# Attention logits computed once, and the probabilities turned by DMA transposes

## The chip, the cores and the metric

The kernel runs on one core of a Trainium2 chip. The metric is device microseconds of that core for one launch; lower is better. Each kernel is run several times, and the median is compared. The profiles show one execution each, in microseconds from its first instruction. The engines are TensorE (PE, with its weight loads as PEld), VectorE (DVE), ScalarE (ACT), GpSimd (POOL) and SyncE (SP), which in this kernel issues all DMA transfers. A queue name with a q (SPq) is an engine's instruction queue.

## What is computed

The reference mixes, per token, a memory-augmented attention and a SwiGLU feed-forward part with a sigmoid gate. There are 2048 tokens, 576 model dimensions, 32 heads of 18 dimensions and 4608 hidden dimensions. Attention is causal within each of four segments of 512 tokens; a running state carries earlier segments.

```python
for s in range(N):                      # N = 4 segments of L = 512
    logits = jnp.einsum("bhqd,bhkd->bhqk", qs, ks) * scale + mask
    p = _softmax(logits, axis=-1)
    a_dot = jnp.einsum("bhqk,bhkd->bhqd", p, vs)
    num = jnp.einsum("bhld,bhde->bhle", pq, M)
    den = jnp.einsum("bhld,bhd->bhl", pq, z)[..., None] + 1e-6
    outs.append(g * num / den + (1.0 - g) * a_dot)
    M = M + jnp.einsum("bhld,bhle->bhde", pk, vs)
    z = z + jnp.einsum("bhld->bhd", pk)
a = o @ wo                              # o: the segments' outputs together
b = (silu(x @ w_gate) * (x @ w_up)) @ w_down
return gate * a + (1 - gate) * b        # gate = sigmoid(x . gate_w)
```

Inputs and output are float32. The kernel reaches this precision with split operands: a number is carried as a high term and one or two low terms of a narrower type, and the products of the terms are added in PSUM.

## The kernel before

A first stage (to about 230 us) makes q, k and v, the state and its reads. It writes q and k, each as three bf16 terms, into a DRAM tensor `stk`, and v into `vd`. The last stage (from about 1710 us) multiplies with `wo` and mixes. Between them runs the feed-forward part, twice through 36 blocks of hidden units: `seven` (L1034 and L1037) makes gate and up products, `down_group` (L893) the down product of three blocks at a time. In the first half the split weights are made (`w_make`) and stored to DRAM (`wc`, `dc`); in the second they are fetched again (`w_fetch` at L703, `d_fetch`).

The softmax attention is woven into these two halves. `att_gen` is a generator; each of its steps (`tau`) issues a few instructions of several stages of a pipeline, and `beat`, called between the feed-forward's products, lets it do a step whenever a credit (`TICK`) has reached one. The order of every engine is the order in which the program issues; there is no scheduler.

A unit `u` is two heads of one segment. Its causal logits, in blocks of 128 x 128, fill five PSUM banks (`SPLAN`, `TPLAN`). `stack_loads` brings its q and k from `stk` with the terms laid out one under another on 108 partitions (`KR`), so that one matmul adds all products of terms. The pipeline of a unit:

- `s_bank` (L727, L734), step 5u+n: logits with queries on the partitions, two heads, and DVE's maximum of each row of a query block into `mb`. With the fifth bank DVE splits the eight columns of maxima, less a shift, into three bf16 terms `mq` (L740 to L743).
- `m_tr` (L748, L750): a matmul with the identity turns `mq`, ACT copies it to `mt`; SP stores it to DRAM (`mxd`, L830) and loads it back as three more rows of `qst` (`row_load`, L193). The same rows of `kst` hold -1.
- `t_bank` (L769, L773, L781), 12 steps behind `s_bank` (`TL`): the logits again, with keys on the partitions and the maxima subtracted by the three rows, 111 partitions deep; ACT takes the exponential of the whole bank, POOL zeroes the masked half of the diagonal blocks.
- two steps later (`PL`) DVE casts the bank to fp16 (`p1`, L861) and POOL subtracts for the low term (`p2`, L863).
- `pv_step` (L798, L800): 40 matmuls per unit, each with a 128 x 128 block of `p1` or `p2` as weights and v's three (two) bf16 terms and the column of ones as moving operand, into one bank; DVE adds the terms (L805).
- `o_step` divides by the row sum and stores the result to `atd`.

The three banks 5, 6 and 7 (`ts_tile`) serve `s_bank`, `t_bank`, `m_tr` and the unit's output in turn. `qst` and `kst` have four buffers each (`NST`), since a unit's q and k are needed until its `t_bank`.

Of the kernel before, what the change touches and what calls it, by code (L numbers as in the profile page):

```python
# [37 lines left out]
NST = 4  # L38
TL = 12
PL = 2  # L40
VL = 3
# [22 lines left out]
def gated_mix(ctx, tc, xT, xrest, wf, wfr, wfh, wd, wv, wo, beta, cmask, ident, bmask, out):  # L64
# [11 lines left out]
    mxd = dram.tile([2 * NB, 3, 8, P], BF, name="mxd")  # L76
# [96 lines left out]
    VP, accs, cur, unit, ms, mts, mbs = {}, {}, {}, {}, {}, {}, []  # L173
# [17 lines left out]

    def row_load(u):
        nc.sync.dma_start(qst[u % NST][KR:KR + 3].rearrange("z j (i n) -> z (j i) n", n=P), mxd[u])  # L193

# [75 lines left out]
    with ExitStack() as st:  # L270
# [314 lines left out]
        for s in range(NSEG):  # L585
# [41 lines left out]
            if s == 3:  # L627
# [4 lines left out]
                for i in range(NST):  # L632
                    if i < 2:
                        qst.append(kq.tile([P, 2, L], BF, name=f"qst{i}"))
                    if i < NST - 1:
                        kst.append(kq.tile([P, 2, L], BF, name=f"kst{i}"))
# [9 lines left out]
            for n in range(8):  # L646
# [10 lines left out]
                else:  # L657
                    if n == 4:
                        wraw_of[1] = [w_load(1, u) for u in range(2)]
                    if n < 2:  # L660
                        first_sum(6, n)
                    elif n < 6:
                        if n < 4:
                            nc.gpsimd.memset(f32(rhs[n - 2][96:]), 0.0)
                        if 3 <= n < 5:
                            r_fetch(n - 3)
                        if n - 2 < len(kst):
                            nc.gpsimd.memset(kst[n - 2], -1.0)
# [13 lines left out]
    with ExitStack() as st:  # L682
# [26 lines left out]
        kst.append(kp.tile([P, 2, L], BF, name=f"kst{NST - 1}", bufs=1))  # L709
        for i in range(2, NST):  # L710
            qst.append(kp.tile([P, 2, L], BF, name=f"qst{i}", bufs=1))
        defer(8, lambda: nc.gpsimd.memset(kst[NST - 1], -1.0))
        idb = kp.tile([P, P], BF, name="idb", bufs=1)
        defer(9, lambda: nc.gpsimd.tensor_copy(idb, idt))
        mqs = [kp.tile([P, P], BF, name=f"mq{i}", bufs=1) for i in range(2)]
        for i in range(2):
            defer(9 + i, lambda i=i: nc.gpsimd.memset(mqs[i], 0.0))
        SPLAN = [[(0, 0, 3)], [(0, 1, 3)], [(384, 0, 0), (0, 0, 2)], [(384, 1, 0), (0, 1, 2)], [(0, 0, 1), (256, 1, 1)]]

        def s_bank(u, n):  # L720
            qs, ks = qst[u % NST], kst[u % NST]
            m = mbs[u % 2]
            bank = SPLAN[n]
            t = ts_tile()
            for c, pr, i in bank:
# [3 lines left out]
                yield  # L729
            for c, pr, i in bank:  # L730
# [3 lines left out]
                nc.vector.tensor_tensor_reduce(scr[:, :w], t[:, c:c + w], cm[:, L - w:L], 1.0, -3.0e38,  # L734
                                               OP.add, OP.max, m[:, k:k + 1])
            if n == 4:
                mq = mqs[u % 2][:, :24].rearrange("p (z q) -> p z q", q=8)
                mr = kp.tile([P, 8], F32, name="mr")
                c = -SHIFT / SCALE
                nc.vector.tensor_scalar_add(mq[:, 0], m, c)  # L740
                nc.vector.scalar_tensor_tensor(mr, m, c, mq[:, 0], op0=OP.add, op1=OP.subtract)
                nc.vector.tensor_copy(mq[:, 1], mr)
                nc.vector.tensor_sub(mq[:, 2], mr, mq[:, 1])  # L743
            yield

        def m_tr(u):
            tr = ts_tile()
            nc.tensor.matmul(tr[:, :P], mqs[u % 2], idb, start=True, stop=True)  # L748
            mt = mts[u] = kp.tile([24, P], BF, name="mt")
            nc.scalar.activation(mt, tr[:24, :P], AF.Copy)  # L750

        def blk(pr, j, i):
            if j == 0:
                return pr, P * i
            if j == 1:
                return 2 + pr, P * (i - 1)
            if j == 3:
                return 2 + pr, 384
            return 4, 256 * pr + P * (i - 2)

        TPLAN = [[(0, 0)], [(1, 0)], [(0, 1), (0, 3)], [(1, 3), (1, 1)], [(0, 2), (1, 2)]]

        def t_bank(u, k):
            qs, ks = qst[u % NST], kst[u % NST]
            t = ts_tile()
            for pr, j in TPLAN[k]:
                _, c = blk(pr, j, j)
                w = L - P * j
                nc.tensor.matmul(t[:, c:c + w], ks[:KR + 3, pr, P * j:P * j + P], qs[:KR + 3, pr, P * j:L],  # L769
                                 start=True, stop=True)  # L770
                yield
            pe = ap.tile([P, L], F32, name="pe", bufs=4)
            nc.scalar.activation(pe, t, AF.Exp, scale=SCALE)  # L773
            if k < 2:
                d = pe[:, 0:P]
                pat = [[1, P]]
            else:
                st_ = 384 if k < 4 else 256
                d = bass.AP(tensor=pe.tensor, offset=pe.offset, ap=[pe.ap[0], [st_, 2], [1, P]])
                pat = [[0, 2], [1, P]]  # L780
            nc.gpsimd.affine_select(d, d, pattern=pat, compare_op=OP.is_ge, fill=0.0, base=0, channel_multiplier=-1)  # L781
            cur[5 * u + k] = pe
            yield

        def pv_step(z):
            u, k = divmod(z, 5)
            g, hf = divmod(u, 2)
            s, b = divmod(u, 16)
            if k == 0:
                unit[u] = ts_tile([P, 2, 4, 3 * E])  # L790
# [32 lines left out]
        def att_gen():  # L823
            N = 10 * NB
            for tau in range(N + TL + VL + 5):
# [26 lines left out]
                if u < 2 * NB:  # L852
                    runs.append(s_bank(u, n))
# [378 lines left out]
```

## Time and profile before

| | us |
|---|---|
| three runs | 1804.73, 1805.08, 1808.49 |
| median | 1805.08 |
| span of the profiled execution | 1803.0 |

The page of the profile gives, per engine, busy time and its share of the span; the chain that ended last, followed back from the last instruction; and the costliest groups of instructions. A row of a group reads: line, engine, operation, output<-input with partitions and elements, count; then busy time and mean duration in ns of one; then the idle time of the engine just before such instructions, and what ended it. Views of a window give the busy time of each engine in it (with the number of instructions in brackets), the granted TensorE clock, the mean share of the 16 DMA engines that was in use, and what they moved.

### The profile page before, as it was taken

How to read it: one execution, taken by the hardware profiler on the slowest of the kernel's cores; microseconds unless marked ns; L12 is line 12 of the kernel's file. 1: busy time of each engine (PE TensorE's matmuls, PEld its weight loads, DVE VectorE, ACT ScalarE, POOL GpSimd, SP SyncE). 2: the span in 40 equal slices, each digit the busy share in tenths (PEclk: the TensorE clock that was granted, in tenths of full speed). 3: DMA queues.
4: the chain of work that ended last, by engine and by line, in shares of the span. 5: the costliest groups of instructions: out<-in, count | busy, mean ns of one | idle time of the engine just before them, and what ended most of it. 6: DMA issues, size and time to landing. Idle time of an engine off the chain costs nothing.

```text
span 1803.0 us, 36363 instructions
## 1 busy us (share of the span) xinstructions
PE 1779.1 (99%) x12444; PEld 1529.7 (85%) x12444; DVE 1269.7 (70%) x3257; ACT 960.0 (53%) x1799; POOL 832.3 (46%) x1065
## 2 busy tenths in 40 slices
PE   9999999999999999999989999999999999999999
PEld 7898978888888888888877888888887887888899
DVE  6566566778877777777777767777777777764455
ACT  7666564465556555655546465355355355354511
POOL 4434632345554455345535555555555555553121
PEclk9999999999999999999999999999999999999999
DMA  8643496777657756776478456466455455456644
GB/s 289 215 174 141 148 324 205 229 260 264 186 198 248 256 181 193 246 247 193 160 262 247 137 176 195 135 172 195 124 179 181 144 168 180 137 160 187 199 137 139
DMA packets 244073, 352.01 MB, mean 195 GB/s; under 512 B 83440, under 2 KB 125680, under 8 KB 243888
## 3 DMA queue, kind: packets, MB, share of 16 engines
q1 hardware_dynamic: 243888, 349.68, 60.3%
q8 instruction: 99, 1.62, 0.4%
q14 instruction: 86, 0.70, 0.1%
HBM read 210.72 MB, written 138.87 MB: 194 GB/s over the span
## 4 chain that ended last, share of the span: by engine, by line
PE 92%; DVE 2%; DMA 2%; ACT 2%; issue 1%; SPq 0%; POOL 0%; ACTq 0%; DVEq 0%
PE bank L1034 36%; PE bank L893 25%; PE bank L138 11%; PE bank L1037 6%; PE bank L769 4%; PE bank L727 4%; PE bank L798 2%; PE bank L800 1%; PE bank L446 1%; PE bank L400 1%; DMA wo__23682<-wc 0%; DVE xo L116 0%; DMA stk<-q 0%; PE bank L332 0%; DMA raw<-in_xT_dram 0%
## 5 line engine op out<-in xcount | busy, mean ns | idle before, releaser
L893 PE MATMUL bank<-dw,hh 128*128 128x320 f32 (+1 forms) x2304 | 486.5, 304 | 6.0 <-DVE ya L898 4.4
L863 POOL TENSOR_TENSOR p<-pe,p 128x512 f16<-128x512 f32 x320 | 382.7, 1196 | 155.5 <-DVE p L861 107.1
L893 PEld LDWEIGHTS bank<-dw,hh 128*128 128x128 f32 x2304 | 377.9, 189 | 24.8 <-DVE ya L898 6.3
L773 ACT ACTIVATE pe<-bank 128x512 f32<-128x512 f32 x320 | 190.3, 595 | 313.9 <-PE bank L769 285.5
L893 PE MATMUL bank<-dw,hl 128*128 128x320 f32 (+1 forms) x1152 | 340.2, 295 | 0.3 <-DVE hl L116 0.3
L781 POOL TENSOR_SCALAR_AFFINE_SELECT pe<-pe 128x256 f32<-128x256 f32 (+1 forms) x320 | 137.5, 430 | 293.7 <-ACT pe L773 289.8
L734 DVE CUSTOM_DVE_ANT_0 scr<-bank,cm 128x512 bf16<-128x512 f32 (+3 forms) x512 | 247.8, 484 | 20.0 <-PE bank L727 12.0
L898 DVE TENSOR_TENSOR ya<-bank,ya 128x320 f32<-128x320 f32 x352 | 157.9, 453 | 113.2 <-PE bank L893 110.8
L893 PEld LDWEIGHTS bank<-dw,hl 128*128 128x128 f32 x1152 | 217.6, 189 | 0.9 <-DVE hl L116 0.9
L1037 PE MATMUL bank<-xr,rh 128*128 128x512 f32 x504 | 196.8, 391 | 0.0
L861 DVE CAST p<-pe 128x512 f16<-128x512 f32 x320 | 152.3, 476 | 0.0
L769 PE MATMUL bank<-qst,kst 111*128 111x512 bf16 (+3 forms) x512 | 150.9, 303 | 0.0
L727 PE MATMUL bank<-kst,qst 108*128 108x512 bf16 (+3 forms) x512 | 126.0, 300 | 0.6 <-DVE mb L734 0.5
L247 POOL TENSOR_TENSOR ws<-raw 128x256 f32<-128x256 f32 x72 | 66.2, 920 | 108.0 <-DMA raw<-in_wf_dram 51.7
L977 DVE TENSOR_TENSOR hl<-row,hh 128x512 fp32r<-128x512 f32 x120 | 99.7, 831 | 18.9 <-ACT hh L976 18.4
L1037 PEld LDWEIGHTS bank<-xr,rh 128*128 128x128 f32 x504 | 94.7, 188 | 20.3
L1101 ACT ACTIVATE row<-bank 128x512 f32<-128x512 f32 x72 | 43.1, 599 | 122.3 <-PE bank L1037 122.3
L1106 DVE TENSOR_TENSOR row<-bank,row 128x512 f32<-128x512 f32 x72 | 49.8, 691 | 81.8 <-ACT bank L1105 81.8
L1116 DVE TENSOR_TENSOR row<-bank,row 128x512 f32<-128x512 f32 x72 | 49.7, 690 | 64.2 <-PE bank L1037 51.5
L1105 ACT ACTIVATE bank<-bank 128x512 f32<-128x512 f32 x72 | 41.9, 582 | 97.9 <-PE bank L1037 94.8
L138 PE MATMUL bank<-xo,qhi 128*128 128x512 f32 x264 | 83.1, 396 | 0.0
L1098 DVE TENSOR_TENSOR bank<-bank,row 128x512 f32<-128x512 f32 x72 | 50.2, 697 | 41.6 <-PE bank L1037 33.4
(1702 smaller groups left out, 4040.3 us busy)
## 6 DMA issues: line engine op xcount, KB each, us to landing
rh<-rc SPq DMA_DIRECT2D x72, 336.0 KB
dc<-dw SPq DMA_DIRECT2D x36, 576.0 KB
dw<-dc SPq DMA_DIRECT2D x36, 576.0 KB
raw<-in_wf_dram SPq DMA_DIRECT2D x72, 256.0 KB
stk<-q SPq DMA_DIRECT2D x32, 384.0 KB
draw<-in_wd_dram SPq DMA_DIRECT2D x36, 288.0 KB
rc<-rt SPq DMA_DIRECT2D x42, 224.0 KB
vd<-vps SPq DMA_DIRECT2D x8, 912.0 KB
```

What stands on the lines that cost most here:

```text
L138: nc.tensor.matmul(t, st[n], mv[n], start=(n == 0), stop=(n == 13))
L727: nc.tensor.matmul(t[:, c:c + w], qs[:KR, pr, P * i:P * i + P], ks[:KR, pr, 0:w], start=True, stop=True)
L734: nc.vector.tensor_tensor_reduce(scr[:, :w], t[:, c:c + w], cm[:, L - w:L], 1.0, -3.0e38, OP.add, OP.max, m[:, k:k + 1])
L769: nc.tensor.matmul(t[:, c:c + w], ks[:KR + 3, pr, P * j:P * j + P], qs[:KR + 3, pr, P * j:L], start=True, stop=True)
L773: nc.scalar.activation(pe, t, AF.Exp, scale=SCALE)
L781: nc.gpsimd.affine_select(d, d, pattern=pat, compare_op=OP.is_ge, fill=0.0, base=0, channel_multiplier=-1)
L861: nc.vector.tensor_copy(p1, pe)
L863: nc.gpsimd.tensor_sub(p2, pe, p1)
L893: nc.tensor.matmul(t, p, q[:, cs], start=(n == 0), stop=(n == 3 * CH - 1))
L898: nc.vector.tensor_add(ya[:, i, cs], t, ya[:, i, cs])
L1034: nc.tensor.matmul(t, w[:, p, z], x[z][:, q], start=first and n == 0, stop=False, skip_group_check=True)
L1037: nc.tensor.matmul(t, rem[:, RPOS[j]], XR[j], start=False, stop=True, skip_group_check=True)
```

## The change

The logits are computed once, with queries on the partitions. DVE now takes, in place of the row maximum, the minimum of -scale x (logit + mask + shift); the shift is folded into the mask on the host. This number is the bias of ACT's exponential (`e_bank`), which is issued one step after the bank's logits, one ACTIVATE for each query block, since each has a bias of its own. POOL's mask and the split into two fp16 terms follow as before, but both terms go into one tile `p` of 128 x 1024. One step after that SP issues a DMA transpose of the whole tile into `pt` (`x_bank`), eight blocks of 128 x 128, SBUF to SBUF. `v_unit` does the 40 matmuls of a unit with blocks of `pt` as weights, three steps after the last transpose of the unit is issued.

`t_bank`, `m_tr`, `row_load`, the split of the maxima, `mxd`, the identity in bf16 and the rows of -1 go away. `qst` and `kst` have two buffers in place of four. `p` has three buffers, `pt` eight. Feed-forward, credits and `stack_loads` are unchanged. The DMA descriptor scratch is reduced from 1024 to 256.

```diff
-NST = 4
-TL = 12
-PL = 2
-VL = 3
+NST = 2
+PL = 3
+XL = 4
+VL = 7
...
-                scr = kp.tile([P, L], BF, name="scr", bufs=1)
-                nc.vector.tensor_tensor_reduce(scr[:, :w], t[:, c:c + w], cm[:, L - w:L], 1.0, -3.0e38,
-                                               OP.add, OP.max, m[:, k:k + 1])
-            if n == 4:
-                mq = mqs[u % 2][:, :24].rearrange("p (z q) -> p z q", q=8)
...
+                nc.vector.tensor_tensor_reduce(scr[:, :w], t[:, c:c + w], cm[:, L - w:L], -SCALE, 3.0e38,
+                                               OP.add, OP.min, m[:, k:k + 1])
+            cur["t", z] = t
+
+        def e_bank(z):
+            u, n = divmod(z, 5)
+            m = mbs[u % 2]
+            t = cur.pop(("t", z))
             pe = ap.tile([P, L], F32, name="pe", bufs=4)
-            nc.scalar.activation(pe, t, AF.Exp, scale=SCALE)
...
+            for c, pr, i in SPLAN[n]:
+                w = P * (i + 1)
+                k = pr * 4 + i
+                nc.scalar.activation(pe[:, c:c + w], t[:, c:c + w], AF.Exp, bias=m[:, k:k + 1], scale=SCALE)
...
+            nc.gpsimd.affine_select(d, d, pattern=pat, compare_op=OP.is_ge, fill=0.0, base=0, channel_multiplier=1)
+            cur["e", z] = pe
+
+        def p_bank(z):
+            pe = cur.pop(("e", z))
+            p = cur["p", z] = ap.tile([P, 2, L], F16, name="p", bufs=3)
+            nc.vector.tensor_copy(p[:, 0], pe)
+            nc.gpsimd.tensor_sub(p[:, 1], pe, p[:, 0])
+
+        def x_bank(z):
+            pt = cur["x", z] = ap.tile([P, 8, P], F16, name="pt", bufs=8)
+            nc.sync.dma_start_transpose(pt, cur.pop(("p", z)).rearrange("p a n -> p (a n)"))
+
+        def v_unit(u):
...
+                pt = cur["x", z]
+                nc.tensor.matmul(t[:, pr, i, :], pt[:, c], v, start=(n == 0), stop=False, skip_group_check=True)
+                nc.tensor.matmul(t[:, pr, i, 0:2 * E], pt[:, 4 + c], v[:, 0:2 * E], start=False,
+                                 stop=(n == len(todo) - 1), skip_group_check=True)
...
+                if 0 <= tau - 1 < N:
+                    e_bank(tau - 1)
                 if z % 5 == 4 and 0 <= z < N:
-                    for k in range(z - 4, z + 1):
-                        pv_step(k)
...
+                    v_unit(z // 5)
+                if tau < N:
+                    s_bank(tau)
+                if 0 <= tau - XL < N:
+                    x_bank(tau - XL)
+                if 0 <= tau - PL < N:
+                    p_bank(tau - PL)
                 yield
```

More of the change, by code (lines that the diff above doesn't have):

```diff
@@ L632, in gated_mix @@
                 for i in range(NST):
[L633 to L636, printed above, removed]
+                    qst.append(kq.tile([P, 2, L], BF, name=f"qst{i}"))
+                    kst.append(kq.tile([P, 2, L], BF, name=f"kst{i}"))
                 for i in range(2):
@@ L809, in gated_mix @@
+            for n in range(5):
+                cur.pop(("x", 5 * u + n))
+            if hf == 0:
+                accs[g] = ap.tile([P, 2, 8, E], F32, name="acc")
+            nc.vector.tensor_reduce(accs[g][:, hf], t.rearrange("p a i (t e) -> p (a i) e t", t=3),
+                                    axis=AX.X, op=OP.add)
         sends = []
@@ L824, in att_gen @@
             N = 10 * NB
-            for tau in range(N + TL + VL + 5):
+            for tau in range(N + VL + 5):
                 u, n = divmod(tau, 5)
```

129 lines of the change are left out of this document (20 added, 109 removed).

## The prediction

> **What bounds the kernel now.** I read the page first, then the chain of waits, then the busy time of the two stages in which the attention runs beside the feed-forward part.
>
> ```profile
> span 1803.0 us, 36363 instructions
> ...
> PE 1779.1 (99%) x12444; PEld 1529.7 (85%) x12444; DVE 1269.7 (70%) x3257; ACT 960.0 (53%) x1799; POOL 832.3 (46%) x1065
> ...
> q1 hardware_dynamic: 243888, 349.68, 60.3%
> ...
> PE 92%; DVE 2%; DMA 2%; ACT 2%; issue 1%; SPq 0%; POOL 0%; ACTq 0%; DVEq 0%
> ```
>
> TensorE is busy for 99% of the span and holds 92% of the chain that ended last, so work taken from it comes off the end as long as nothing else takes its place. The next resource is the 16 DMA engines, 60.3% filled by the one queue that SP issues.
>
> ```profile
> by line: PE bank L1034 36.4%; PE bank L893 24.7%; PE bank L138 10.7%; PE bank L1037 6.0%; PE bank L769 4.0%; PE bank L727 3.9%; PE bank L798 2.3%; PE bank L800 1.3%; PE bank L446 0.9%; PE bank L400 0.8%; issue 0.8%; DMA wo__23682<-wc 0.5%;
> ```
>
> This is the chain by line. L769, the second set of logits, which the change removes, holds 4.0% of it. That is the figure to use: the groups give L769 150.9 us of busy time, but matmuls overlap in the records, and the chain counts only the time until the next one starts.
>
> ```profile
> 393.00:868.40 475.40, 475.40 (x3252) 412.10 (x3248) 364.45 (x898) 272.28 (x537) 232.60 (x308) 1.00 0.67 221
> 955.10:1590.90 635.80, 635.60 (x5003) 525.22 (x5003) 471.08 (x1385) 331.01 (x560) 342.49 (x440) 1.00 0.56 169
> ...
> 393.00:868.40 475.40, 31.51 (x128) 12.64 (x128) 1.00 0.67 221
> 955.10:1590.90 635.80, 78.77 (x320) 31.58 (x319) 1.00 0.56 169
> ```
>
> These are two windows, one in each half of the feed-forward part, first all engines (PE, PEld, DVE, ACT, POOL, granted clock, DMA share, GB/s), then L727 alone. A unit (one pair of head pairs, five banks) has eight L727 matmuls, so the first window holds 128/8 = 16 units, one in 475.4/16 = 29.7 us, and the second 320/8 = 40 units, one in 15.9 us. PE is full in both and the clock is fully granted. The DMA engines do 0.67 x 29.7 = 19.9 us of work per unit in the first rhythm and 0.56 x 15.9 = 8.9 us in the second. I count 24 of the 64 units at the first rhythm and 40 at the second.
>
> **What the change takes away.** L769 goes: 4.0% of 1803.0 is 72.1 us. The small matmul that turns the row maxima goes too:
>
> ```profile
> 1596.19 0.23 PE L748 MATMUL bank<-idb,mq 128*128 128x128 bf16 x1
> 1596.26 0.28 PE L769 MATMUL bank<-qst,kst 111*128 111x256 bf16 x1
> ```
>
> The next matmul starts 0.07 us behind it, and there are 64, so 4.5 us. Together TensorE loses 76.6 us, 1.20 us per unit. Nothing else of TensorE changes in amount: the matmuls with V are the same 40 per unit, with the turned tile as weights in place of p.
>
> ```profile
> L773 ACT ACTIVATE pe<-bank 128x512 f32<-128x512 f32 x320 | 190.3, 595 | 313.9 <-PE bank L769 285.5 <-PE bank L727 21.2 <-POOL p L863 6.2
> ...
> L750 ACT ACTIVATE mt<-bank 24x128 bf16<-24x128 f32 x64 | 16.7, 261 | 59.8 <-PE bank L748 59.8
> L740 DVE TENSOR_SCALAR mq<-mb 128x8 bf16<-128x8 f32 x64 | 14.1, 220 | 2.2
> ...
> L375 ACT ACTIVATE vps<-bank 128x288 bf16<-128x288 f32 x32 | 13.3, 417 | 0.0
> ...
> L741 DVE SCALAR_TENSOR_TENSOR mr<-mb,mq 128x8 f32<-128x8 f32 x64 | 12.8, 201 | 2.2
> L742 DVE CAST mq<-mr 128x8 bf16<-128x8 f32 x64 | 11.7, 183 | 2.2
> L743 DVE TENSOR_TENSOR mq<-mr,mq 128x8 bf16<-128x8 f32 x64 | 11.2, 175 | 2.2
> ```
>
> The bias is one number per partition and differs from block to block, so five exponentials of 512 columns a unit become eight: two of 512 columns (595 ns each), two of 384, two of 256 and two of 128. By the rows of 512 and of 288 columns (417 ns) and that of 128 (261 ns) I put them at 595, 490, 395 and 261 ns: 3.48 us a unit, against 5 x 595 + 261 = 3.24 us. The 15 us that ACT gains over 64 units cost nothing: in the second window it works 331.0 of 635.8 us. DVE loses the four small steps (220 + 201 + 183 + 175 ns, 0.78 us a unit, 50 us in all); it bounds nothing, so this brings nothing. The cast to fp16, the mask and the subtraction for the low term keep their counts.
>
> One wait is new on ACT: the exponentials now wait for DVE's minimum of their own bank, and behind them on ACT stand the copies that free the feed-forward's banks.
>
> ```profile
> 803.82 0.27 PE L727 MATMUL bank<-kst,qst 108*128 108x256 bf16 x1
> ...
> 805.17 0.08 DVE L734 DVE_READ_ACCUMULATOR2_ANT mb<- 128x1 f32 x1
> ```
>
> DVE has the result 805.25 - 803.82 = 1.4 us after the matmul starts, and the change issues the exponential a step later, 15.9/5 = 3.2 us behind. I cost it at nothing. If DVE were a step late, ACT and then PE would wait up to those 3.2 us, at most a fifth of the second rhythm; nothing in the trace has DVE that late.
>
> **What it adds: 320 DMA transposes.** Each turns a 128 x 1024 fp16 tile, 262,144 bytes, from SBUF to SBUF. The trace has no such transfer, so both its prices, on the 16 engines and on SP, are bounded by rows. A run of the destination, or of a source row for one 128-column block, is 256 bytes. The nearest row is a stretch in which only 256-byte pieces move:
>
> ```profile
> DMA  0000000000001699999999999999999999999999
> GB/s 0 0 0 0 0 0 0 0 0 0 0 0 41 154 241 236 230 225 215 195 200 220 195 220 205 230 225 251 241 220 210 225 190 225 200 210 220 220 210 225
> DMA packets 1164, 0.29 MB, mean 147 GB/s; under 512 B 1164, under 2 KB 1164, under 8 KB 1164
> ...
> 490.00:512.00 22.00, 22.00 (x147) 18.81 (x146) 16.73 (x37) 14.55 (x31) 7.82 (x12) 1.00 0.97 369
> 845.00:868.00 23.00, 23.00 (x137) 19.44 (x136) 17.03 (x37) 15.49 (x33) 7.36 (x9) 1.00 0.97 347
> ```
>
> The first three lines are the DMA view of 808.8 to 810.8 us, in 40 slices: with all engines full, 256-byte pieces run at about 217 GB/s. The other two are windows filled with larger pieces, 369 GB/s at a share of 0.97; they also show that the engines can be held at 0.97 for 22 us while PE stays full, so I take 0.97 as the most that can be used. Prices for one transpose: 262,144 B / (369/0.97) = 0.69 us of all engines as a copy of large pieces; 262,144 / 217 GB/s = 1.21 us as a copy of 256-byte pieces; twice that, 2.42 us, if a block must be read whole in such pieces before it is written in such pieces, without overlap. Beyond it the trace gives no limit: an element goes from one partition to another alone, and at the worst each of the 131,072 is a packet, 1.21 x 128 = 155 us. I take 1.8 us, midway between the row of 256-byte pieces and its double, since in a transpose neither side is a plain run and some of the reading must come before the writing. The two small DMAs that go (6 KB each, per unit) are under 1% of this.
>
> The sum per unit at 1.8 us, five transposes: first rhythm (19.9 + 9.0)/0.97 = 29.8 us against 29.7 before, +0.1, over 24 units +2 us. Second rhythm (8.9 + 9.0)/0.97 = 18.5 us against 15.9, +2.6, over 40 units +104 us. The engines become the bound in the second half, the 76.6 us of TensorE are swallowed, and the span is 1803.0 + 106 = 1909 us. The median of the runs lies 2.1 us above the profiled span: **1911 us**. Who waits: TensorE, at the first weights of a unit's matmuls with V, three steps (3 x 3.2 = 9.5 us) after the last of the five transposes is issued; all feed-forward matmuls stand behind it on its queue.
>
> [...] What follows from a cheap transpose is the first rival.
>
> SP must issue the 320 as well, in order among its other transfers.
>
> ```profile
> L835 SPq DMA_DIRECT2D qst<-stk x315: 283/771/1343, 283.4 to 1589.8; - x158
> L835 SPq DMA_DIRECT2D kst<-stk x315: 278/487/1413, 284.2 to 1590.7; - x158
> ...
> L230 SPq DMA_DIRECT2D rc<-rt x42: 540/572/1536, 278.2 to 818.4; - x42
> ...
> L830 SPq DMA_DIRECT2D mxd<-mt x64: 300/312/964, 297.5 to 1614.8; - x64
> ...
> L193 SPq DMA_DIRECT2D qst<-mxd x64: 252/365/442, 329.4 to 1616.2; - x64
> ...
> 1206.60 0.34 SPq L703 DMA_DIRECT2D wo__16507<-wc  x1
> ```
>
> Columns: shortest, median and longest issue in ns. A unit costs SP 5 x 0.771 + 5 x 0.487 = 6.3 us for the stacks, 0.31 + 0.37 for the maxima, and in the second half 36 x 9 weight fetches over 40 units, 8.1 x 0.34 = 2.8 us: 9.8 us of 15.9. The maxima go: 9.1. L230 issues 896 runs of 256 bytes in 572 ns; 1024 runs are then 0.65 us, and SP has 9.1 + 3.3 = 12.4 us of work per unit, which hides. The bounds are 0.30 us (the shortest L830) and 1.54 us (the longest L230), where SP has 9.1 + 7.7 = 16.8 us. I take 0.65. Each issue also waits for POOL's low term of the step before, and weight fetches queue behind it; POOL works 342 of 635.8 us, so I add nothing.
>
> **Rivals.**
> 1. **The transposes hide.** At 1.21 us or less: first rhythm (19.9 + 6.05)/0.97 = 26.8 us, under the 28.5 us that TensorE then needs; second (8.9 + 6.05)/0.97 = 15.4 us. 24 x 1.2 + 40 x 0.5 = 49 us less: 1756 us. At 0.69 us PE bounds everywhere: 1805 - 77 = 1728 us. For it: DMA at 0.97 did not starve PE, and there are nine microseconds of slack. Against: it needs transposes at the speed of copies. The forecast turns into this one at about 1.45 us, where the second half's loss (40 x 0.7) equals the first half's gain.
> 2. **The transposes cost twice the small copies.** At 2.42 us: (19.9 + 12.1)/0.97 = 33.0, +3.3 x 24 = 79; (8.9 + 12.1)/0.97 = 21.6, +5.7 x 40 = 230; 2114 us, and 330 us more for each further microsecond. For it: element-wise scatter and no row that excludes it. Against: nothing but the lack of a row.
> 3. **SP's issue becomes the bound.** It decides in the second half from (15.9 - 9.1)/5 = 1.36 us per issue. At the longest row, 1.54 us, it gives 40 x 0.9 - 29 = +7, so 1812 us; at double that, 3.1 us, 24.6 us a unit and some 2150 us. [...]
> 4. **They cancel**: within 0.2% (3.6 us, about what a measurement can tell) of 1805 us, with a transpose near 1.45 us.
>
> **How the numbers follow.** Forecast (the DMA engines bind, 1810 to 2050 us, its own range): 0.37. Hidden: 0.34. Twice the cost or more: 0.18. SP: 0.07, nearly all of it slower. Cancel: 0.04. So faster 0.35, same 0.04, slower 0.61. The range goes from 1728 us, the lower end, to 2450 us, which is a transpose of 3.4 us; what lies outside is some 0.05 below and 0.1 above.
>
> **What would show it.** Right: no L769 row, PE under 95% in the second half, its longest waits at the first weights of the matmuls with V, on a DMA; DMA share above 0.9 in the second half; the chain holding DMA. Wrong: DMA share under 0.85 with PE still full (rival 1), SP's issue of a transpose over 1.4 us with DMA engines below 0.85 (rival 3), or ACT waiting for DVE's minimum and PE for ACT.

## The result, and the profile after

| | before | after |
|---|---|---|
| median of the runs | 1804.90 us (1803.23 to 1808.49, 4 runs) | 1972.25 us (1968.59 to 1976.86, 4 runs) |
| span of the profiled execution | 1803.0 us | 1967.6 us |
| ratio | | 1.0929, interval 1.0906 to 1.0952 |

The change makes the kernel 9.3% slower. The page of the changed kernel, first its engines, its one busy queue (packets, MB, share of the 16 engines' span) and the chain by engine:

```profile
span 1967.6 us, 35841 instructions
...
PE 1777.4 (90%) x11868; PEld 1516.8 (77%) x11868; DVE 1222.8 (62%) x3001; ACT 999.6 (51%) x1927; POOL 824.3 (42%) x1058
...
q1 hardware_dynamic: 579120, 432.82, 80.8%
...
PE 51%; DMA 22%; DVE 8%; issue 6%; ACT 5%; SPq 4%; POOL 4%; DVEq 0%; ACTq 0%; POOLq 0%
```

TensorE fell from 99% of the span to 90%, and from 92% of the chain to 51%. What took its place is a mixture: DMA, DVE, POOL and "issue". The two windows of the prediction, cut at the same units (the first matmul of units 4, 20, 23 and 63), first all engines and then L710 alone, which was L727:

```profile
401.60:906.50 504.90, 472.05 (x3099) 407.18 (x3098) 354.21 (x834) 282.33 (x571) 229.80 (x310) 0.98 0.88 249
990.00:1756.20 766.20, 644.21 (x4645) 522.95 (x4644) 442.11 (x1223) 355.81 (x642) 342.63 (x442) 0.95 0.87 208
...
401.60:906.50 504.90, 31.65 (x129) 8.70 (x129) 0.98 0.88 249
990.00:1756.20 766.20, 79.87 (x320) 21.88 (x320) 0.95 0.87 208
```

Sixteen units now take 504.9 us, 31.6 us each (29.7 before), and forty take 766.2 us, 19.2 us each (15.9 before). The edges of the windows say where the time went. Against before, unit 4 starts 8.6 us later (401.6 - 393.0), unit 20 38.1, unit 23 34.9, unit 63 165.3, and the span ends 164.6 us later. So the first half lost 35 us, the second 130, and the rest nothing. In the second window TensorE works 644.2 of 766.2 us, 84%. The DMA engines stand at 0.87 and are not full.

The waits of this kernel (engine, line, what it waited for, us in total, times, longest):

```profile
POOL p L743 <- DVE p L742: 476.9, 260, 4.9
DVE p L742 <- DMA pt<-p: 302.0, 132, 5.4
ACT pe L728 <- DVE mb L716: 240.4, 99, 6.1
...
PEld L758 <- DMA pt<-p: 59.0, 34, 4.0
PE bank L758 <- DMA pt<-p: 55.5, 34, 3.9
```

The longest is POOL's, whose subtraction waits for DVE's cast of the same bank. The next is DVE's: its cast into one of the three buffers of `p` waits until a transpose has read that buffer. TensorE's longest row is at L758, the matmuls with V. But the fetched weights (`wo<-wc`) stand in the view one by one, each under a number of its own. Added up over the second window, TensorE waits 41 us for them and 40 us at the V matmuls, of 121 us in all. SP issues these fetches too. Why the transposes are late is not in this view. It is in SP's timeline; here 7 us of it (start, duration of the issue):

```profile
1311.56 1.23 SPq L747 DMA_TRANSPOSE pt<-p  x1
1312.88 0.80 SPq L790 DMA_DIRECT2D qst<-stk  x1
1313.73 0.48 SPq L790 DMA_DIRECT2D kst<-stk  x1
1314.27 0.77 SPq L790 DMA_DIRECT2D qst<-stk  x1
1315.09 0.75 SPq L790 DMA_DIRECT2D kst<-stk  x1
1315.94 0.42 SPq L790 DMA_DIRECT2D qst<-stk  x1
1316.41 0.31 SPq L790 DMA_DIRECT2D kst<-stk  x1
1316.83 1.27 SPq L747 DMA_TRANSPOSE pt<-p  x1
1318.14 0.59 SPq L695 DMA_DIRECT2D wo__16137<-wc  x1
```

One issue follows the other at 0.04 to 0.11 us: 1311.56 + 1.23 = 1312.79, and the next starts at 1312.88. Before, the same queue stood idle for microseconds at a time in its own second half:

```profile
1212.01 0.58 SPq L197 DMA_DIRECT2D v<-vd  x1
1217.23 0.31 SPq L830 DMA_DIRECT2D mxd<-mt  x1
```

And the chain of the changed kernel goes through that queue, and from it into the ring of `p` (start, duration, what):

```profile
1316.41 0.31 SPq L790
1316.72 0.05 issue
1316.83 3.14 DMA pt<-p
...
1320.06 0.44 DVE p L742
...
1320.57 1.16 POOL p L743
1321.73 0.09 POOL pe L736
1321.82 3.25 DMA pt<-p
...
1325.12 0.20 PE bank L758
```

By this chain a transpose lands 3.14 us after its issue starts. Then come the cast, the low term, the next transpose (3.25 us), and only then TensorE's matmul. That leaves three suspects, and they are all late together: SP's queue, the 16 engines, and the ring of three buffers.

SP's rows of the second window, by line (shortest, median and longest issue in ns):

```profile
L790 SPq DMA_DIRECT2D qst<-stk x200: 411/776/1823, 989.7 to 1756.0; - x100
L790 SPq DMA_DIRECT2D kst<-stk x199: 283/487/1345, 990.5 to 1752.8; - x199
...
L747 SPq DMA_TRANSPOSE pt<-p x200: 1231/1267/3547, 991.3 to 1754.0; - x100
```

A transpose holds SP for 1.27 us, where the prediction had 0.65. Adding up the durations of all 890 issues of this window gives 691 us of 766, 90%; gaps under 0.15 us between them add 64 us, 8%. Only 20 gaps are longer, 11 us together. Before, the issues filled 62% of the second window (397 of 636 us), and 107 longer gaps left 195 us.

### The profile page after: what moved, and what is told of

Its sections match the earlier page's. It is cut to its first block, busy times and chain, and to the rows that moved or that the text cites. A ratio compares the mean times of both kernels' runs of the same rounds, so it can differ in the third digit from the quotient of the medians.

```text
span 1967.6 us, 35841 instructions
## 1 busy us (share of the span) xinstructions
PE 1777.4 (90%) x11868; PEld 1516.8 (77%) x11868; DVE 1222.8 (62%) x3001; ACT 999.6 (51%) x1927; POOL 824.3 (42%) x1058
## 3 DMA queue, kind: packets, MB, share of 16 engines
q1 hardware_dynamic: 579120, 432.82, 80.8%
q8 instruction: 94, 1.54, 0.3%
## 4 chain that ended last, share of the span: by engine, by line
PE 51%; DMA 22%; DVE 8%; issue 6%; ACT 5%; SPq 4%; POOL 4%; DVEq 0%; ACTq 0%; POOLq 0%
PE bank L975 21%; DMA pt<-p 15%; PE bank L834 13%; PE bank L137 8%; PE bank L978 3%; POOL p L743 2%; DMA draw<-in_wd_dram 2%; DVE p L742 2%; PE bank L710 2%; SPq L790 1%; SPq L747 1%; DVE ya L839 1%; PE bank L758 1%; DVE scr L716 1%; ACT L968 1%
## 5 line engine op out<-in xcount | busy, mean ns | idle before, releaser
L834 PE MATMUL bank<-dw,hh 128*128 128x320 f32 (+1 forms) x2304 | 496.0, 308 | 33.1 <-DVE ya L839 27.3
L728 ACT ACTIVATE pe<-bank,mb 128x512 f32<-128x512 f32 (+3 forms) x512 | 244.9, 523 | 284.1 <-DVE mb L716 240.4
L742 DVE CAST p<-pe 128x512 f16<-128x512 f32 x320 | 141.5, 442 | 303.8 <-DMA pt<-p 302.0
L716 DVE CUSTOM_DVE_ANT_0 scr<-bank,cm 128x512 bf16<-128x512 f32 (+3 forms) x512 | 246.2, 481 | 10.3 <-PE bank L710 3.4
L978 PE MATMUL bank<-xr,rh 128*128 128x512 f32 x504 | 202.2, 401 | 9.2 <-DMA rh<-rc 9.1
L736 POOL TENSOR_SCALAR_AFFINE_SELECT pe<-pe 128x256 f32<-128x256 f32 (+1 forms) x320 | 145.2, 454 | 105.0 <-ACT pe L728 103.0
L758 PE MATMUL bank<-v,pt 128*128 128x57 bf16 x1280 | 83.5, 190 | 55.5 <-DMA pt<-p 55.5
L710 PE MATMUL bank<-kst,qst 108*128 108x512 bf16 (+3 forms) x512 | 127.3, 310 | 3.7 <-DMA kst<-stk 2.8
L758 PEld LDWEIGHTS <-pt 128*128 128x128 f16 x1280 | 72.3, 97 | 70.1 <-DMA pt<-p 59.0
L918 DVE TENSOR_TENSOR hl<-row,hh 128x512 fp32r<-128x512 f32 x120 | 106.6, 888 | 20.9 <-ACT hh L917 20.5
L1032 ACT ACTIVATE bank<-bank 128x512 f32<-128x512 f32 x72 | 41.9, 581 | 131.3 <-PE bank L978 122.5
L1046 ACT ACTIVATE bank<-bank 128x512 f32<-128x512 f32 x72 | 41.9, 583 | 121.9 <-PE bank L978 121.6
L1047 DVE TENSOR_TENSOR row<-bank,row 128x512 f32<-128x512 f32 x72 | 49.6, 689 | 59.2 <-ACT bank L1046 59.2
```

The lines of the kernel that those rows point to most:

```text
L710: nc.tensor.matmul(t[:, c:c + w], qs[:KR, pr, P * i:P * i + P], ks[:KR, pr, 0:w], start=True, stop=True)
L728: nc.scalar.activation(pe[:, c:c + w], t[:, c:c + w], AF.Exp, bias=m[:, k:k + 1], scale=SCALE)
L742: nc.vector.tensor_copy(p[:, 0], pe)
L758: nc.tensor.matmul(t[:, pr, i, :], pt[:, c], v, start=(n == 0), stop=False, skip_group_check=True)
L834: nc.tensor.matmul(t, p, q[:, cs], start=(n == 0), stop=(n == 3 * CH - 1))
L978: nc.tensor.matmul(t, rem[:, RPOS[j]], XR[j], start=False, stop=True, skip_group_check=True)
```

## The experiments

All are edits of the changed kernel unless said otherwise. Ratios are against the kernel before, which was measured beside each of them (medians of 1803.6 to 1805.7 us). The table gives, for most of the kernels, us per unit in the two windows, cut at the same units as above; share of the DMA engines; and SP's time in issue, added up from its rows, as a share of the second window.

| kernel | median us | first | second | DMA, second | SP in issue, second |
|---|---|---|---|---|---|
| before | 1804.9 | 29.7 | 15.9 | 0.56 | 0.62 |
| after | 1972.3 | 31.6 | 19.2 | 0.87 | 0.90 |
| e1_none | 1731.7 | 28.8 | 14.7 | 0.60 | 0.64 |
| e4_unread | 1963.0 | 31.4 | 19.2 | 0.88 | 0.91 |
| e2_act_loads | 1922.7 | 29.6 | 19.0 | 0.94 | 0.57 |
| e3_copy | 1823.2 | 29.3 | 16.6 | 0.76 | 0.77 |
| e3_copy256 | 1887.4 | 30.0 | 17.9 | 0.82 | 0.85 |
| e6_issue_only | 2292.3 | 36.5 | 24.5 | 0.44 | 0.89 |
| e8_high_only | 1912.7 | 30.6 | 18.4 | 0.72 | 0.90 |
| e11_high_pairs | 1770.2 | 28.8 | 15.8 | 0.81 | 0.85 |
| e12_two_loads | 1759.0 | 28.9 | 15.2 | 0.99 | 0.76 |

With the gaps under 0.15 us counted in, SP's share is 0.99 in the changed kernel, e4, e6 and e8, 0.93 in e3_copy256 and e11, and 0.81 in e12.

**No transposes.** The V matmuls read `p` itself.

```diff
-            p = cur["p", z] = ap.tile([P, 2, L], F16, name="p", bufs=3)
+            p = cur["p", z] = ap.tile([P, 2, L], F16, name="p", bufs=11)
...
-            pt = cur["x", z] = ap.tile([P, 8, P], F16, name="pt", bufs=8)
-            nc.sync.dma_start_transpose(pt, cur.pop(("p", z)).rearrange("p a n -> p (a n)"))
+            cur["x", z] = cur.pop(("p", z)).rearrange("p a (c n) -> p (a c) n", n=P)
```

> The changed kernel without the transposes: the matmuls with V take blocks of the unturned p as weights, with the same waits on DVE and POOL, and p has 11 buffers. All theories expect the gain of the removed matmuls alone: 1805 - 77 = 1728 us, 1720 to 1745. If it stays above 1760, something else of the change costs time, such as the exponentials that wait for DVE's minimum, or the smaller exponentials.

Measured: 1731.7 us, ratio 0.9601 (0.9573 to 0.9629). From its page, and then one of its waits:

```profile
PE 1704.5 (98%) x11868; PEld 1487.1 (86%) x11868; DVE 1233.8 (71%) x3001; ACT 994.7 (57%) x1927; POOL 829.5 (48%) x1058
...
q1 hardware_dynamic: 241200, 348.89, 62.7%
```

```profile
ACT pe L728 <- DVE mb L716: 175.0, 92, 3.5
```

TensorE is the bound again and works 1779.1 - 1704.5 = 74.6 us less than before. Everything in the change but the transposes therefore costs nothing at the end, ACT's new wait among it: 175 us of it stand beside a TensorE that is 98% busy. The whole loss, 1972 - 1732 = 240 us, is the transposes'. One thing more differs. For the same matmuls of the second window TensorE is busy 589.0 us here, at a granted clock of 1.00, and 644.2 us in the changed kernel, at 0.95. In e12 below, which has all the transposes, the clock is 1.00 again. So the lower clock does not come from the transposes alone. It is seen where TensorE waits: 0.98 in e3_copy, where TensorE is idle for 663.1 - 611.0 = 52 us of the second window, and 0.86 in e6, where it is for 981.4 - 696.7 = 285 us. No run shows it as a cause of the loss.

**Transposes issued, nobody reads them.** This takes away TensorE's wait for them, and eases the ring (eight buffers of `p`).

```diff
-            p = cur["p", z] = ap.tile([P, 2, L], F16, name="p", bufs=3)
+            p = cur["p", z] = ap.tile([P, 2, L], F16, name="p", bufs=8)
...
-            pt = cur["x", z] = ap.tile([P, 8, P], F16, name="pt", bufs=8)
-            nc.sync.dma_start_transpose(pt, cur.pop(("p", z)).rearrange("p a n -> p (a n)"))
+            p = cur.pop(("p", z))
+            cur["x", z] = p.rearrange("p a (c n) -> p (a c) n", n=P)
+            pt = ap.tile([P, 8, P], F16, name="pt", bufs=3)
+            nc.sync.dma_start_transpose(pt, p.rearrange("p a n -> p (a n)"))
```

> The changed kernel with the transposes issued as before but read by nobody: the matmuls with V take the unturned p, p has 8 buffers, the turned tiles 3. SP's issue and the DMA traffic are those of the change, but neither DVE nor PE waits for a turned tile until p comes round eight banks later. If the short ring of p (3 buffers) and the wait of PE for turned tiles make the loss, it falls to 1740 to 1780 us. If SP's issue or the DMA engines make it, it stays within 30 us of the changed kernel: 1940 to 1985 us.

Measured: 1963.0 us, 1.0884 (1.0852 to 1.0915), 9 us under the changed kernel. TensorE's waits in it:

```profile
PE bank L710 <- DMA kst<-stk: 54.0, 34, 4.3
PE bank L980 <- DMA rh<-rc: 27.7, 10, 5.4
```

The wait for the turned tile is gone, and TensorE waits as long for something else that SP issues: the stacks of q and k (L710) and the split weights (L980). So the 302 us of DVE and the wait at L758 are consequences, not the limit. Whatever is next in SP's order is late.

**The stacks' loads on ACT's queue**, to relieve SP, once with the transposes read and once without (e5 is e4 with the same edit).

```diff
-                        nc.sync.dma_start(*d)
+                        nc.scalar.dma_start(*d)
```

> The changed kernel with the ten loads of a unit's q and k (630 of them, 0.65 us of issue each, 6.3 us a unit) issued by ACT in place of SP. Same bytes on the DMA engines. If SP's issue is the bound (it is in issue for 90% of the second half, with 8% more in the small gaps between issues), the second rhythm falls from 18.7 us a unit to what the DMA engines allow, (8.9 + 7.9)/0.97 = 17.3 us, and the whole to 1870 to 1900 us. If the DMA engines are the bound, it stays at 1960 to 1985 us. If the three buffers of p are (DVE's cast waits 302 us for transposes), it falls only as far as the transposes are issued sooner: 1920 to 1960 us.

> The kernel with unread transposes and eight buffers of p, and the loads of q and k issued by ACT. If SP's issue is the bound: 1790 to 1880 us, and the DMA share of the second half rises above 0.92. If the DMA engines are: 1940 us or more. If the ring of p is: as with SP's loads, 1740 to 1780 us.

Measured: 1922.7 us, 1.0660 (1.0629 to 1.0691), and 1922.5 us, 1.0659 (1.0628 to 1.0690). The windows of e2 and two of its waits:

```profile
392.80:866.50 473.70, 462.55 (x3099) 402.18 (x3098) 354.29 (x834) 280.10 (x571) 233.33 (x310) 1.00 0.98 266
949.80:1711.30 761.50, 641.29 (x4645) 526.75 (x4645) 452.42 (x1224) 352.79 (x641) 334.59 (x440) 0.93 0.94 210
```

```profile
ACT pe L728 <- DMA qst<-stk: 184.9, 46, 7.9
...
ACT pe L728 <- DMA kst<-stk: 88.1, 22, 7.5
```

The first half is back at 473.7/16 = 29.6 us a unit. The second is not, and SP isn't full there any more. But now ACT is held: its exponentials stand behind the loads it has to issue, 273 us of waits that were not there. In the second window ACT is in issue for 258 us, and 110 of TensorE's 120 us of waits are for ACT. So the second half of these two says nothing for or against SP. The time of e2 lies in the range that was expected if the three buffers of `p` were the limit; but with eight buffers and nobody reading, e5 takes the same time, so they are not.

**Plain copies in place of the transposes**: of 2 KB per partition, then in runs of 256 bytes, then the first with the loads on ACT as a control for e2. The V matmuls wait for the copy as they did for the turned tile.

```diff
-            nc.sync.dma_start_transpose(pt, cur.pop(("p", z)).rearrange("p a n -> p (a n)"))
+            nc.sync.dma_start(pt.rearrange("p a n -> p (a n)"), cur.pop(("p", z)).rearrange("p a n -> p (a n)"))
```

```diff
-            pt = cur["x", z] = ap.tile([P, 8, P], F16, name="pt", bufs=8)
-            nc.sync.dma_start_transpose(pt, cur.pop(("p", z)).rearrange("p a n -> p (a n)"))
+            pt = cur["x", z] = ap.tile([P, 8, P + 2], F16, name="pt", bufs=8)
+            nc.sync.dma_start(pt[:, :, :P], cur.pop(("p", z)).rearrange("p h (a n) -> p (h a) n", n=P))
...
```

> The changed kernel with each transpose replaced by a plain copy of the same tile, 2 KB a partition, so the matmuls with V take the unturned p; the wait for the landed tile and the rings stay. Same bytes, an issue of about 0.4 us, and by the packets of 2 KB (95 ns for one) 0.76 us of the DMA engines per copy in place of 1.6. If bytes alone made the loss it would stay above 1900 us. By the sum with 0.76 us, (8.9 + 3.8)/0.97 = 13.1 us, TensorE bounds: 1732 to 1750 us. More than 1760 would put the rest on the wait for the landed tile.

> The changed kernel with each transpose replaced by a plain copy in runs of 256 bytes, 1024 of them as the transpose has (the target has 4 bytes of padding between runs; the matmuls with V take the unturned p). This is the row from which the price was taken: 1.21 us of all engines per copy at 217 GB/s. If the transpose costs what 256-byte pieces cost, this kernel is as slow in DMA as the change, and only SP is relieved: 1880 to 1960 us. If the transposing itself costs more, the sum with 1.21 us gives (8.9 + 6.05)/0.97 = 15.4 us in the second half: 1740 to 1780 us.

> Plain copies of 2 KB per partition in place of the transposes (the matmuls with V take the unturned p), and the loads of q and k issued by ACT. Against the kernel with transposes and loads on ACT (1922.7 us, 19.0 us a unit in the second half) only the price of the transfer on the DMA engines and its issue differ. If the DMA engines hold that kernel, this one falls to 1735 to 1770 us. If ACT's issuing holds it, this one stays at 1900 us or more.

Measured: 1823.2 us, 1.0104 (1.0059 to 1.0149); 1887.4 us, 1.0459 (1.0429 to 1.0490); 1872.9 us, 1.0375 (1.0348 to 1.0401). What one copy costs SP, and the page's row of the busy queue, for the first and then for the second:

```profile
L747 SPq DMA_DIRECT2D pt<-p x320: 464/534/1616, 288.4 to 1637.5; - x160
```

```profile
q1 hardware_dynamic: 287280, 432.80, 72.5%
```

```profile
L747 SPq DMA_DIRECT2D pt<-p x320: 593/653/1633, 288.3 to 1705.5; - x160
```

```profile
q1 hardware_dynamic: 574000, 432.80, 76.6%
```

The plain copy was expected not to be felt and was: some 90 us over e1, although its second window shows 0.76 for the engines and 0.77 for SP, neither full. In that window TensorE waits 49 us, of which 28 are for weight fetches and 14 for the copy at the V matmuls. By the view of SP's waits, SP waits 53 us there, at its copies, for POOL, and the fetches stand behind these in its order. That is a lead, but no run tests it, and the cause stays open. The second kernel lies in the range that was expected if a transpose cost the engines what such a copy does. Its queue says otherwise: the copy is the cheaper one, 1.13 us of the engines against 1.58, as worked out below. The 0.65 us that the prediction took for an issue is exactly what a copy in 256-byte runs takes (653 ns); a transpose of the same bytes takes 1.27. The third run lies between its two expected values. It shows what ACT pays: the same copies are 50 us slower once ACT issues the loads, and ACT's exponentials wait 188 us behind the loads of `qst`.

**Issues without data.** Four tiny copies a bank (4 KB each) in place of the transpose; the V matmuls read `p`, which has ten buffers.

```diff
-            p = cur["p", z] = ap.tile([P, 2, L], F16, name="p", bufs=3)
+            p = cur["p", z] = ap.tile([P, 2, L], F16, name="p", bufs=10)
...
-            pt = cur["x", z] = ap.tile([P, 8, P], F16, name="pt", bufs=8)
-            nc.sync.dma_start_transpose(pt, cur.pop(("p", z)).rearrange("p a n -> p (a n)"))
+            p = cur.pop(("p", z))
+            cur["x", z] = p.rearrange("p a (c n) -> p (a c) n", n=P)
+            pt = ap.tile([P, 4, 16], F16, name="pt", bufs=3)
+            for k in range(4):
+                nc.sync.dma_start(pt[:, k], p[:, 1, P * k:P * k + 16])
```

> The kernel without transposes (the matmuls with V take the unturned p), and in place of each transpose SP issues four copies of 32 bytes per partition, behind the same wait for POOL: four issues of about 0.32 us with the gaps between them, 1.3 to 1.6 us, as long as a transpose's 1.27, but under 0.1 us of the DMA engines. If SP's issue is a bound by itself, SP has 9.1 + 7.5 us and its gaps, some 17.5 us a unit in the second half against 14.7 that TensorE needs: 1800 to 1860 us. If the DMA engines make the loss, SP's issue hides: 1731 to 1760 us.

Measured: 2292.3 us, 1.2703 (1.2666 to 1.2740). The row of the copies and the second window:

```profile
L750 SPq DMA_DIRECT2D pt<-p x1280: 464/596/1871, 288.4 to 2115.3; - x183
```

```profile
1093.60:2075.00 981.40, 696.66 (x4646) 564.31 (x4646) 441.49 (x1225) 358.32 (x645) 337.24 (x444) 0.86 0.44 113
```

Four issues take 4 x 0.60 = 2.4 us, nearly twice a transpose's, more than was meant, so this is an overdose. It still shows the mechanism by itself: with the DMA engines at 0.44, SP at 89% in issue (99% with the gaps) sets a rhythm of 981.4/40 = 24.5 us.

**Half the data, as many transposes; then half the data and half the transposes.** In both only the high term is turned. In the first a transpose is 128 x 512, one per bank. In the second two banks share one of 128 x 1024.

```diff
-            nc.gpsimd.tensor_sub(p[:, 1], pe, p[:, 0])
...
-            pt = cur["x", z] = ap.tile([P, 8, P], F16, name="pt", bufs=8)
-            nc.sync.dma_start_transpose(pt, cur.pop(("p", z)).rearrange("p a n -> p (a n)"))
+            pt = cur["x", z] = ap.tile([P, 4, P], F16, name="pt", bufs=8)
+            nc.sync.dma_start_transpose(pt, cur.pop(("p", z))[:, 0])
...
-                nc.tensor.matmul(t[:, pr, i, 0:2 * E], pt[:, 4 + c], v[:, 0:2 * E], start=False,
-                                 stop=(n == len(todo) - 1), skip_group_check=True)
```

```diff
-VL = 7
+VL = 8
...
+            if z % 2 == 0:
+                cur["p", z // 2] = ap.tile([P, 2, L], F16, name="p", bufs=3)
+            nc.vector.tensor_copy(cur["p", z // 2][:, z % 2], pe)
...
+            if z % 2:
+                pt = cur["x", z // 2] = ap.tile([P, 8, P], F16, name="pt", bufs=6)
+                nc.sync.dma_start_transpose(pt, cur.pop(("p", z // 2)).rearrange("p a n -> p (a n)"))
...
```

> The changed kernel with the high fp16 term alone: the low term, its POOL subtraction and its 20 matmuls a unit are left out, so each transpose has half the size. If SP and the DMA engines are proportional to size, SP needs 9.1 + 3.3 us and the DMA engines (8.9 + 3.9)/0.97 = 13.2 us a unit in the second half, under TensorE's 14: 1690 to 1730 us. If a transpose has a large fixed cost, it stays above 1800 us.

> The high fp16 term alone, and one transpose of 128 x 1024 for two banks in place of two of 128 x 512, one step more of lag; SP issues everything. Same bytes on the DMA engines as the high term alone. An issue took 1.23 us for 512 columns and 1.27 for 1024, so SP saves 2.5 x 1.2 = 3.0 us a unit. If SP's issue is the limit, the second half falls from 18.4 to about 15.3 us a unit and the first from 30.6 to about 29: 1760 to 1800 us. If the DMA engines or the wait for the tile are, it stays at 1890 to 1920 us.

Measured: 1912.7 us, 1.0599 (1.0559 to 1.0640), and 1770.2 us, 0.9812 (0.9794 to 0.9831). The transposes' row and the second window of the first, then of the second:

```profile
L746 SPq DMA_TRANSPOSE pt<-p x320: 1188/1221/2627, 287.6 to 1727.5; - x160
```

```profile
966.30:1700.50 734.20, 623.78 (x3845) 504.42 (x3845) 414.39 (x1223) 355.07 (x641) 98.16 (x241) 0.95 0.72 181
```

```profile
L748 SPq DMA_TRANSPOSE pt<-p x160: 1237/1279/3920, 289.2 to 1588.6; - x160
```

```profile
928.90:1560.80 631.90, 587.83 (x3846) 487.42 (x3846) 423.11 (x1225) 354.62 (x644) 99.39 (x241) 0.98 0.81 210
```

This pair decides. Half the bytes cost SP 1.22 us a transpose against 1.27, nearly the same. With the engines down to 0.72 the unit still takes 18.4 us, and SP is at 90%. Then the same bytes in half as many transposes: the engines do the same work (0.72 x 18.4 = 13.2 us a unit, 0.81 x 15.8 = 12.8), SP is down to 85%, and the kernel is 142 us faster. The second also gives `p` twice the banks and the V matmuls a step more; by e4 an eased ring is worth some 9 us, where nobody reads the transposes. With the low term left out it is faster than the kernel before. The full computation with two banks to a transpose was not tried.

The first of the two, with the loads on ACT:

```diff
-                        nc.sync.dma_start(*d)
+                        nc.scalar.dma_start(*d)
```

> The high fp16 term alone (the low term, its subtraction and its 20 matmuls a unit left out) and the loads of q and k issued by ACT: both suspected limits relieved together. With the high term alone the time was 1912.7 us with SP in issue for 90% of the second half (18.4 us a unit) and a DMA share of 0.72; with the loads on ACT alone 1922.7 us with a DMA share of 0.93. If SP's issue is the first limit and the DMA engines the second, the two together fall to what TensorE allows: 1700 to 1745 us, DMA share about 0.8 with PE above 97% in the second half. If what the loads on ACT left behind is ACT itself, held up by issuing them, it stays at 1850 us or more. If the wait for a landed turned tile is the limit, 1800 us or more.

Measured: 1850.2 us, 1.0235 (1.0211 to 1.0260), 62 us under e8. Its waits have ACT held by the loads again:

```profile
ACT pe L728 <- DMA qst<-stk: 232.8, 62, 8.7
```

The time lies where it was expected if ACT's issuing holds the kernel up, and these waits agree, as in e10. So it does not decide between SP and the engines.

**SP relieved and no other engine loaded.** All transposes as in the changed kernel; the stacks are loaded for the first two units alone, and 620 loads fall away.

```diff
-                if n in (2, 3) and u + 1 < 2 * NB:
+                if n in (2, 3) and u + 1 < NST:
```

> The changed kernel with q and k loaded for the first two units alone; all later units compute with these, so 620 loads are left out. Both fp16 terms are turned as in the change. SP is relieved of 6.4 us of issue a unit without a load on ACT; the DMA engines of 432 pieces of 1 KB a unit, by 55 ns a piece 1.5 us. If SP's issue is the one limit, TensorE bounds next: 14.7 us a unit in the second half, 1730 to 1750 us. If the DMA engines come right behind, they have 0.87 x 19.2 - 1.5 = 15.2 us, at 0.97 15.7 us a unit: 1760 to 1790 us and a share above 0.93. If the DMA engines were the limit at the share of 0.87 that the changed kernel has, 15.2/0.87 = 17.5 us a unit and 1870 to 1900 us. If the three buffers of p were, it stays above 1920 us.

Measured: 1759.0 us, 0.9753 (0.9678 to 0.9828). Its windows:

```profile
388.30:851.20 462.90, 459.54 (x3098) 401.87 (x3097) 349.48 (x834) 280.84 (x571) 234.95 (x310) 1.00 0.94 257
933.70:1542.70 609.00, 594.22 (x4645) 498.40 (x4644) 446.58 (x1222) 354.45 (x640) 344.01 (x441) 1.00 0.99 231
```

With SP at 76% the transposes are all done and TensorE is full in the first half (459.5 of 462.9 us) and nearly so in the second. There the engines are at 0.99, and a unit takes 609.0/40 = 15.2 us, half a microsecond over e1's 14.7. So the engines are the next limit, right behind SP. Full engines did not lengthen SP's issues in these runs either. Here, at 0.99, a transpose takes SP this long (second window, ns):

```profile
L747 SPq DMA_TRANSPOSE pt<-p x200: 1231/1236/4210, 934.3 to 1541.0; - x100
```

The median is 1.24 us, against 1.27 in the changed kernel at 0.87. And in e6, with the engines at 0.44, the stacks' loads take 0.82 and 0.48 us at the median, against 0.78 and 0.49.

This run takes the loads' DMA work away too, some 1.6 us a unit (16.7 - 15.1, from 0.87 x 19.2 and 0.99 x 15.2), so by itself it doesn't part SP from the engines; e8, e11 and e6 do.

## Why the prediction was right in its sign and wrong in its cause

- **TensorE's 76.6 us: right.** e1 gives 74.6 us, and 1731.7 us against the 1728 that the prediction had for transposes at no cost.
- **ACT and DVE at nothing: right**, by e1. One size was off: ACT's exponentials take 684, 578, 471 and 361 ns by width where 595, 490, 395 and 261 were put, so ACT gained 40 us (960.0 to 999.6), not 15. DVE lost 47 (1269.7 to 1222.8) of the 50 forecast.
- **A transpose's price on the 16 engines: about right.** The busy queue's time is 0.808 x 1967.6 = 1590 us after, 0.627 x 1730.7 = 1085 in e1; (1590 - 1085)/320 = 1.58 us, where 1.8 was taken. By the same sum a copy in 256-byte runs is (0.766 x 1886.7 - 1085)/320 = 1.13 us, near the row's 1.21. A transpose was not as cheap as a copy in this kernel: its 262,144 bytes in 1.58 us are 166 GB/s, while a plain copy in 2 KB runs took (0.725 x 1817.9 - 1085)/320 = 0.73 us, 359 GB/s.
- **"The DMA engines become the bound": the step that failed.** They stood at 0.87, not over 0.9. At 16.7 us of work a unit they would, at the share of 0.99 that e12 reached, have allowed 16.9 us, 1.0 over before; measured are 3.3 over. What bound the kernel in their place is the next point. The kernel reached neither the 18.5 us forecast for the second half nor the 29.8 for the first.
- **"SP has 12.4 us of work per unit, which hides": wrong, and this is the cause.** SP's second window has 691/40 = 17.3 us of issue and 64/40 = 1.6 us of short gaps a unit. Transposes are 279/40 = 7.0 us in place of 3.3: 1.27 us at the median, some longer (26 of 200 took over 1.5 us, and no run shows why). All other issues are 10.3 us in place of 9.1, mostly because a weight fetch takes 0.53 us at the median, where the prediction had 0.34; the stores of `atd` and loads of `v`, which it left out, are another 0.4. The gaps were not counted at all. These three, 3.7 + 1.2 + 1.6, lift 12.4 to 18.9 of the 19.2 us measured.
- **Rival 3 was the right one, with a chance of 0.07.** Its point, 1.36 us an issue, was too high for the same reason: (15.9 - 10.3 - 1.6)/5 = 0.8 us an issue would have been the point. So 1.27 us fell under a threshold that stood too high, and the sign that was to show the rival (issue over 1.4 us, engines under 0.85) was missed narrowly on both counts. The bounds themselves held the value (0.30 to 1.54). 0.65 us was taken by likeness to a plain DMA with as many runs, and a transpose turned out to cost SP twice that. With half the columns (e8) the issue fell only from 1.27 to 1.22 us.
- **First half +0.1 a unit: wrong**, +1.9. SP is in issue for 417 of its 504.9 us there (83%, added up from its rows), unevenly. Relieve it and the half is back at 29.6 (e2) or 28.9 us (e12), with the engines at 0.98 and 0.94. So their fullness was not the reason.
- **"Each issue also waits for POOL's low term … I add nothing": no harm shown** in the changed kernel. The view of SP's waits puts 80 us down to POOL at L747 in the second window. But the gaps over 0.15 us are 11 us together, and the transposes' records lie only 25 us in all above their median, so hardly more than 36 of 766 us can be waiting. In e3_copy, where SP is not full, the waits for POOL are the lead named above.
- **The signs.** No L769, TensorE under 95% in the second half, its longest waits at the V matmuls on a DMA, the chain holding DMA: all came true, the longest waits only row by row, since the weight fetches add up to as much. None of them could tell the engines from the queue that feeds them. The chain could not either: it gives SPq 4%, and it counts a transpose from the start of its issue as DMA, as at 1316.83. Only the two shares could.

The sum for the span, 1909 us, is 59 us short of the measured one: 33 us of it are the first half (+2 forecast, +35 measured), 26 the second (+104, +130). That the second half came so near is partly luck. A price on the engines somewhat too high stood in for a queue left out.

What stays open: how the last microsecond a unit divides between SP, at 0.99 with its gaps, and the engines, at 0.87; and why plain copies, with SP at 0.77 and the engines at 0.76, cost 90 us.

## What to carry to other kernels

Count the issuing queue like an engine: for each transfer its issue time plus the gap behind it, summed per period against the rhythm (here 17.3 + 1.6 of 19.2 us), before asking how full the DMA engines are (0.87). The two sizes of transpose measured here, one twice the other, cost that queue nearly the same (1.22 and 1.27 us), so fewer and larger ones were cheaper for it. When a wait on a DMA appears, take the wait away once: in e4 that gained 9 us of 240, and other transfers from the same queue were late instead, so the limit was that queue or what stands behind it, not that transfer. Moving issues to another engine is to be weighed against that engine's own work: the same ten loads a unit on ACT gained 50 us in one kernel here and cost 50 in another.

## What the runs showed of the hardware that was not expected

- SP is held 1.22 us by a DMA transpose of 128 x 512 fp16 and 1.27 by one of 128 x 1024, against 0.53 for a plain copy of the larger tile, 0.65 for one in 256-byte runs, and 0.60 for a copy of 4 KB, issued four in a row.
- A transpose of 128 x 1024 fp16 takes 1.58 us of all 16 engines, a copy of the same bytes in 256-byte runs 1.13, and one in 2 KB runs 0.73. The first two each add about 1050 packets to the queue: (579120 - 241200)/320 = 1056 and (574000 - 241200)/320 = 1040.
- Between back-to-back issues lie 0.04 to 0.14 us, 0.07 at the mean (64 us in 869 gaps of the second window), which at 22 issues a unit is 1.6 us.
- Moving 10 loads a unit from SP to ACT cost the kernel with plain copies 50 us (1823 to 1873), since ACT's own work waits behind its issues (its exponentials 188 us behind the loads of `qst`). In the changed kernel, where SP stands at 0.99 with its gaps, the same move gained 50 us (1972 to 1923). There the issue of a transpose takes 1.27 us beside 3.1 to 3.3 us to landing in the chain shown.
